# One weight half instead of three is split between the routing and the first expert, and after that expert's rows

## The chip, the cores and the metric

One core of one Trainium2 chip runs the whole program as one launch. The metric is the device time of that core in microseconds. The kernel before was timed three times: 524.74, 525.13 and 525.47 us, with a median of 525.13 us. One further execution was profiled.

## The reference, cut to what matters

```
attn: per head h, block of 64:  out = (q k^T * D) v + (q * lam^(i+1)) S ;  S = lam^64 S + (k * lam^(63-j))^T v
x     = attn as 1536 rows of 512
moe : e(t) = argmax(x w_gate), g = softmax weight of e(t);   row t = g * relu(x w1[e]) w2[e]     (8 experts, 512 -> 1024 -> 512)
moe2: out = (sigmoid(x w_g) * (x w_v)) w_out                                                     (512 -> 1536 -> 512)
```

All inputs are float32. The output is 1536 rows of 512.

## The kernel before, in words

The program has three stages: the attention with the routing, the eight experts, and the gated MLP. Each engine runs its own instructions in the order in which the program text issues them (`manual_schedule`, line 75), so the place of a call in the text sets the place of its instructions on every engine at once.

**Matmuls in fp16 pairs.** Every float32 factor of the expert stage is split into a high and a low fp16 part, and a product is three matmuls: high by high, low by high, and high by low. A weight therefore has to be split before TensorE can use it. A *chunk* is a quarter of one expert's weights (two chunks of `w1`, two of `w2`, four to an expert), and the program splits a chunk in two *halves* of 128 x 1024. Half n belongs to chunk n // 2, and expert e uses halves 8e to 8e+7, in this order. One half costs one operation on ScalarE, `hi` (line 170), one on VectorE, `lo` (line 171), and a load of 512 KB into one of five staging buffers `st` on SyncE's queue (line 150). The load of half n+5 is issued when `lo` of half n has ended (`wload`, lines 141 to 152).

**Who issues the splits.** `work32` (line 193) issues the next half of the queue. Halves 0 and 1 go into the attention loop at steps 8 and 9 (`T32`). `NB` halves are issued at line 713, between the routing and the first expert. After that, `weights()` (line 232) issues one half at each of nine places of an expert: after each of the four passes of its first layer, after `xtr_e` of the next expert, and twice in each of the two passes of its second layer. `need` (line 237) issues a half on the spot only if the program has not yet issued it; it does not look at whether it has ended. Eight buffers of `hi` and `lo` limit how far ahead the splits run (`usable`).

**One expert.** A pass of the first layer (lines 814 to 832, four of them) is 24 matmuls into a PSUM bank: for each of two output blocks, four with `hi`, four with `lo`, four with `hi` against the low part of the rows. ScalarE then writes `hh` and VectorE `hl`. Passes one and two use the first chunk, three and four the second. Then `xtr_e` (line 687) turns the next expert's rows: eight transposes on TensorE, two casts `xh` on ScalarE, two subtractions `xl` on VectorE. A pass of the second layer (lines 842 to 863, two of them) runs over f = 0 to 7 with three matmuls each (`hi`, `hi`, `lo`), first for one output block and then for another; f = 0 to 3 use the expert's third chunk and f = 4 to 7 its fourth, a half for each two f. ScalarE writes `yh` and VectorE `yl`.

**Around the change.** The routing ends with the lists of rows `gidx` (line 656). `gather(0)` (line 657) fetches the first expert's rows from DRAM by two indirect DMAs on GpSimd's queue, while VectorE finishes the gate weights and builds two diagonal matrices `diag` (line 712). Then come the three splits of line 713, then `xtr_e(0, diag)`, whose matmuls at line 703 turn the rows and apply the gates, and `gather(1)`. Lines 763 to 807 follow: some thirty small VectorE operations that order the six further experts by size and write the table `tab`. SyncE reads the experts' numbers from it (line 808) before it issues a load of a half of expert 2 or later. In expert 1, after its four passes, VectorE also runs `places()` and `further()` (lines 718 to 760).

Of the kernel before, what the change touches and what calls it, by code (L numbers as in the profile page):

```python
# [32 lines left out]
def kernel(  # L33
# [34 lines left out]

    T32, T64, TW, TE = (8, 9), 7, 6, 3

    NB, WARM = 3, (30, 14, 8, 20, 24)

    N64, N64G = 57, 3

# [118 lines left out]
    def work32():  # L193
        return start32()()
# [52 lines left out]
    def bank(kind, shape, name):  # L247
        turns[kind].append(turns[kind].pop(0))
        tag, bufs = turns[kind][-1]
        return ps.tile(shape, F32, tag=tag, bufs=bufs, name=name)  # L250
# [4 lines left out]
    def gather(e):  # L255
        if e < E:
            xg_t[e] = xgp.tile([128, 2, DM], F32, tag="xg", name="xg")
            for r, n in ((0, 128), (1, W[e] - 128)):
                nc.gpsimd.indirect_dma_start(
                    out=xg_t[e][0:n, r, :], out_offset=None, in_=rows_d[:, :],  # L260
                    in_offset=IndirectOffsetOnAxis(ap=gidx[0:n, r, e:e + 1], axis=0))
# [412 lines left out]
    with ExitStack() as mctx:  # L674
# [12 lines left out]
        def xtr_e(e, diag=None):  # L687
            if e >= E:
                return
            xg = xg_t.pop(e)  # L690
            n = W[e] - 128
            xps_t = []
            xh_t[e] = xw_p.tile([128, KD, C], F16, tag="xh", name="xh")[:, :, 0:W[e]]
            xl_t[e] = xw_p.tile([128, KD, C], F16, tag="xl", name="xl")[:, :, 0:W[e]]
            for c2 in range(KD // 2):
                xps_t.append(bank("x", [128, 2, C], "xps_e")[:, :, 0:W[e]])
            for r, k in ((0, 128), (1, n)):
                for c in range(KD):
                    x, y = xg[0:k, r, c * 128:(c + 1) * 128], xps_t[c // 2][:, c % 2, r * 128:r * 128 + k]
                    if diag is None:  # L700
                        nc.tensor.transpose(y, x, ident[0:k, 0:k])
                    else:
                        nc.tensor.matmul(y, lhsT=x, rhs=diag[0:k, r, 0:k], start=True, stop=True)
            for c2, xps in enumerate(xps_t):
                sl = slice(2 * c2, 2 * c2 + 2)
                nc.scalar.copy(xh_t[e][:, sl], xps)
                nc.vector.tensor_tensor(xl_t[e][:, sl], xps, xh_t[e][:, sl], op=ALU.subtract)


        diag = ct.tile([128, 2, 128], F32, name="diag")  # L710
        for r in range(2):
            nc.vector.tensor_scalar(out=diag[:, r], in0=ident, scalar1=gts[:, r, 0:1], scalar2=None, op0=ALU.mult)
        for _ in range(NB):
            work32()
        xtr_e(0, diag)
        gather(1)

        def places():

# [291 lines left out]
```

## Time and profile before

| | |
|---|---|
| median of three runs | 525.13 us |
| profiled execution, its own time | 523.29 us |
| its span, first to last instruction | 521.7 us |
| TensorE (PE) busy | 504.3 us, 97% |
| VectorE (DVE) busy | 306.7 us, 59% |
| ScalarE (ACT) busy | 222.5 us, 43% |
| GpSimd (POOL) busy | 69.9 us, 13% |

The profiled execution took 1.84 us less than the median, and 1.6 us of its time lie outside the span. Engines work side by side, so a busy share does not say what an operation costs. What counts is which engine waited for which, and when. PE's weight loads are listed apart as PEld, and an engine's sequencer as PEq, SPq and so on. A row of a timeline gives the start and the duration; the records of neighbours on one engine overlap by about a tenth of a microsecond, so the distance between starts says what one costs its engine.

### The profile page before, as it was taken

The page shows a single profiled execution, that of the slowest core. Times are in us where ns is not written, and L with a number is a line of the kernel's source. Part 1 is how long each engine was busy: PE and PEld are TensorE (multiplying, and loading weights), DVE is VectorE, ACT ScalarE, POOL GpSimd, SP SyncE. Part 2 cuts the span into 40 slices and gives each one's busy share as a digit, 9 for nine tenths or more (in the row PEclk, how much of TensorE's full clock was granted, in tenths as well). Part 3 has the DMA queues.
Part 4 walks back from the last instruction along what each step waited for, and adds up shares of the span by engine and source line. Part 5 has one row for each costly group of instructions (what it writes and reads, how often), then busy time and mean ns, then how long its engine had stood idle before and what let it go on. Part 6 is the DMA issues. An engine that isn't in the chain of part 4 may idle for free.

```text
span 521.7 us, 9789 instructions
## 1 busy us (share of the span) xinstructions
PE 504.3 (97%) x4013; PEld 338.8 (65%) x4014; DVE 306.7 (59%) x505; ACT 222.5 (43%) x328; POOL 69.9 (13%) x78
## 2 busy tenths in 40 slices
PE   7999997999999999979999999999999999999995
PEld 6888877999999999974444444444444444444442
DVE  5657867979978887853767766677677520000000
ACT  3554643865876787531533334443444310000000
POOL 3576414301201100000000000000000001101101
PEclk9999999999999999998999999999999999999999
DMA  9999965775989787220432222422340001001001
GB/s 171 211 235 276 299 229 192 223 259 188 322 278 322 265 282 240 79 87 1 136 107 82 83 78 92 151 82 80 92 151 1 0 1 40 26 35 41 34 28 40
DMA packets 67472, 72.28 MB, mean 139 GB/s; under 512 B 40218, under 2 KB 40218, under 8 KB 67424
## 3 DMA queue, kind: packets, MB, share of 16 engines
q1 hardware_dynamic: 65072, 65.04, 41.0%
q0 software_dynamic: 2208, 6.57, 3.6%
q8 instruction: 33, 0.54, 0.4%
q14 instruction: 15, 0.12, 0.1%
q10 hardware_dynamic: 144, 0.00, 0.0%
HBM read 65.31 MB, written 6.29 MB: 137 GB/s over the span
## 4 chain that ended last, share of the span: by engine, by line
PE 52%; issue 1%; DMA 1%; POOLq 0%; ACT 0%; ACTq 0%
PE gv_ps L956 36%; PE o_ps L975 16%; DMA out_dram<-osb,oidx 1%; POOLq L1006 0%; ACT osb L978 0%; ACTq L978 0%; POOLq L979 0%
## 5 line engine op out<-in xcount | busy, mean ns | idle before, releaser
L956 PEld LDWEIGHTS <-hi 128*128 128x128 f16 x576 | 56.4, 98 | 71.2 <-issue 3.6
L171 DVE SCALAR_TENSOR_TENSOR lo<-st,hi 128x1024 f16<-128x1024 f32 x64 | 77.8, 1233 | 13.8 <-ACT hi L170 13.7
L956 PE MATMUL gv_ps<-yh,hi 128*128 128x512 f16 x288 | 74.7, 382 | 3.0 <-PEq L872 3.0
L956 PE MATMUL gv_ps<-yh,lo 128*128 128x512 f16 x288 | 74.4, 381 | 0.0
L956 PE MATMUL gv_ps<-yl,hi 128*128 128x512 f16 x288 | 73.9, 379 | 0.0
L170 ACT ACTIVATE hi<-st 128x1024 f16<-128x1024 f32 x64 | 66.2, 1053 | 3.5 <-DMA st<-in_moe_w_dram 3.5
L851 PE MATMUL y_ps<-hl,hi 128*128 128x224 f16 (+6 forms) x256 | 64.6, 253 | 0.3 <-DVE hl L827 0.3
L851 PE MATMUL y_ps<-hh,hi 128*128 128x224 f16 (+6 forms) x256 | 64.6, 253 | 0.0
L851 PE MATMUL y_ps<-hh,lo 128*128 128x224 f16 (+6 forms) x256 | 64.6, 253 | 0.0
L979 POOL DMA_INDIRECT out_dram<-osb,oidx x12 | 11.7, 974 | 329.4 <-ACT osb L978 329.4
L975 PE MATMUL o_ps<-hi,uh 128*128 128x512 f16 x144 | 54.6, 379 | 0.0
L975 PE MATMUL o_ps<-lo,uh 128*128 128x512 f16 x144 | 54.6, 379 | 0.0
L975 PE MATMUL o_ps<-hi,ul 128*128 128x512 f16 x144 | 54.6, 379 | 0.0
L964 ACT CAST uh<-u 128x512 f16<-128x512 f32 x36 | 22.3, 618 | 70.4 <-DVE u L963 70.4
L956 PEld LDWEIGHTS <-lo 128*128 128x128 f16 x288 | 28.4, 99 | 34.6 <-issue 1.1
L975 PEld LDWEIGHTS <-uh 128*128 128x128 f16 x288 | 28.2, 98 | 34.0
L851 PEld LDWEIGHTS <-hi 128*128 128x128 f16 x512 | 47.7, 98 | 0.2
L823 PEld LDWEIGHTS <-hi 128*128 128x128 f16 x512 | 46.4, 98 | 0.7 <-issue 0.6
L978 ACT ACTIVATE osb<-o_ps 128x512 f32<-128x512 f32 x12 | 7.2, 597 | 85.3 <-PE o_ps L975 85.3
L965 DVE TENSOR_TENSOR ul<-u,uh 128x512 f16<-128x512 f32 x36 | 24.9, 692 | 24.6 <-ACT uh L964 24.6
L963 DVE SCALAR_TENSOR_TENSOR u<-gv_ps,sg 128x512 f32<-128x512 f32 x36 | 24.7, 687 | 23.6 <-PE gv_ps L956 18.6
L170 ACT ACTIVATE hi<-cv 128x1024 f16<-128x1024 f32 x18 | 19.0, 1055 | 35.0 <-DVE cv L219 35.0
(168 smaller groups left out, 725.3 us busy)
## 6 DMA issues: line engine op xcount, KB each, us to landing
st<-in_moe_w_dram SPq DMA_DIRECT2D x64, 512.0 KB, 5.5
st<-in_moe_w_gate_dram SPq DMA_DIRECT2D x6, 1024.0 KB, 5.3
st<-in_moe_w_val_dram SPq DMA_DIRECT2D x6, 1024.0 KB, 5.2
st<-in_moe_w_out_dram SPq DMA_DIRECT2D x6, 1024.0 KB, 4.9
q<-in_q_dram SPq DMA_DIRECT2D x12, 256.0 KB, 4.8
k<-in_k_dram SPq DMA_DIRECT2D x12, 256.0 KB, 5.1
v<-in_v_dram SPq DMA_DIRECT2D x12, 256.0 KB, 5.3
rows_d<-X SPq DMA_DIRECT2D x12, 256.0 KB, 4.9
```

The source lines that it names most:

```text
L170: nc.scalar.activation(out=hi, in_=w, func=AF.Copy, scale=SW)
L171: return lambda: nc.vector.scalar_tensor_tensor(out=lo, in0=w, scalar=SW, in1=hi, op0=ALU.mult, op1=ALU.subtract)
L823: nc.tensor.matmul(hp[:, j], lhsT=lw[w][:, c, fs], rhs=rx[:, c], start=(c == 0 and m == 0), stop=(c == KD - 1 and m == 2))
L851: nc.tensor.matmul(yp[:, j], lhsT=lw[w][:, f % 4, ds], rhs=rh[:, f], start=(f == 0 and m == 0), stop=(f == KF - 1 and m == 2))
L956: nc.tensor.matmul(p, lhsT=lw[w][:, c, fs], rhs=ry[:, c, ts], start=(c == 0 and m == 0), stop=(c == KD - 1 and m == 2))
L963: nc.vector.scalar_tensor_tensor(out=u, in0=banks[1], scalar=SU, in1=sg, op0=ALU.mult, op1=ALU.mult)
L964: nc.scalar.copy(uh[:, f, ts], u)
L965: nc.vector.tensor_tensor(ul[:, f, ts], u, uh[:, f, ts], op=ALU.subtract)
L975: nc.tensor.matmul(op, lhsT=lu[:, f, tsl], rhs=rw[w][:, f % 4, :], start=(f == 0 and m == 0), stop=(f == KF2 - 1 and m == 2))
L978: nc.scalar.activation(out=osb, in_=op, func=AF.Copy, scale=1.0 / (SX * SW * SW * SY * SW * SU * SW))
L979: nc.gpsimd.indirect_dma_start(out=out, out_offset=IndirectOffsetOnAxis(ap=oidx[:, t:t + 1], axis=0), in_=osb, in_offset=None)
```

## The change

`NB`, the number of halves split between the routing and the first expert, goes from 3 to 1. The one that is left is issued behind `xtr_e(0, diag)` and `gather(1)`, not ahead of them. Everything else stays, so all later places issue a half that stands two earlier in the queue.

```diff
-    NB, WARM = 3, (30, 14, 8, 20, 24)
+    NB, WARM = 1, (30, 14, 8, 20, 24)
...
         diag = ct.tile([128, 2, 128], F32, name="diag")
         for r in range(2):
             nc.vector.tensor_scalar(out=diag[:, r], in0=ident, scalar1=gts[:, r, 0:1], scalar2=None, op0=ALU.mult)
+        xtr_e(0, diag)
+        gather(1)
         for _ in range(NB):
             work32()
-        xtr_e(0, diag)
-        gather(1)
```

## Rows read from the trace of the kernel before

**Rows 1.** Busy time by engine, 88 to 108 us: length, PE, PEld, DVE, ACT, POOL.
```profile
88.00:108.00 20.00, 20.00 (x210) 20.00 (x210) 17.50 (x46) 13.21 (x19) 4.61 (x4) 1.00 0.80 261
```
**Rows 2.** Waits of PE: who waited for whom, us in total, times, longest.
```profile
PE gv_ps L956 <- PEq L872: 3.0, 1, 3.0
PE xps_e L703 <- DVE lo L171: 1.9, 2, 1.0
...
PE y_ps L851 <- DVE hl L827: 0.3, 1, 0.3
```
**Rows 3.** Timeline of PE, first experts: start, duration, operation, count, idle before it.
```profile
84.17 1.13 PE L703 MATMUL xps_e<-diag,xg 128*128 128x128 f32 x8 [0.97 <-DVE lo L171]
86.22 1.10 PE L703 MATMUL xps_e<-diag,xg 96*128 96x96 f32 x8 [0.92 <-DVE lo L171]
87.49 0.80 PE L823 MATMUL h_ps<-xh,hi 128*128 128x224 f16 x4 [0.17 <-ACT xh L706]
...
92.35 0.55 PE L823 MATMUL h_ps<-xh,hi 128*128 128x224 f16 x4
...
96.95 0.93 PE L701 MATMUL xps_e<-ident,xg 128*128 128x128 f32 x8
...
116.12 0.96 PE L701 MATMUL xps_e<-ident,xg 128*128 128x128 f32 x8
...
126.11 0.56 PE L823 MATMUL h_ps<-xh,hi 128*128 128x232 f16 x4
```
**Rows 4.** Timeline of DVE, the same stretch.
```profile
82.65 3.49 DVE L171 SCALAR_TENSOR_TENSOR lo<-st,hi 128x1024 f16<-128x1024 f32 x3
87.47 1.16 DVE L707 TENSOR_TENSOR xl<-xps_e,xh 128x448 f16<-128x448 f32 x2 [1.34 <-ACT xh L706]
88.55 0.16 DVE L764 SCALAR_TENSOR_TENSOR key<-cnt_s,c 128x6 f32<-128x6 f32 x1
...
92.41 0.62 DVE L827 SCALAR_TENSOR_TENSOR hl<-h_ps,hh 128x448 f16<-128x448 f32 x1
92.94 1.22 DVE L171 SCALAR_TENSOR_TENSOR lo<-st,hi 128x1024 f16<-128x1024 f32 x1
...
117.84 1.25 DVE L171 SCALAR_TENSOR_TENSOR lo<-st,hi 128x1024 f16<-128x1024 f32 x1
119.01 0.25 DVE L721 TENSOR_TENSOR cp<-oh_all,off_x 128x96 f32<-128x96 f16 x1
...
125.16 1.18 DVE L707 TENSOR_TENSOR xl<-xps_e,xh 128x464 f16<-128x464 f32 x2
126.25 2.35 DVE L171 SCALAR_TENSOR_TENSOR lo<-st,hi 128x1024 f16<-128x1024 f32 x2
```
**Rows 5.** Timeline of ACT, the same stretch.
```profile
86.91 0.98 ACT L706 CAST xh<-xps_e 128x448 f16<-128x448 f32 x2 [6.51 <-PE xps_e L703]
...
97.15 0.54 ACT L826 ACTIVATE hh<-h_ps 128x448 f16<-128x448 f32 x1 [0.52 <-PE h_ps L823]
97.59 1.05 ACT L170 ACTIVATE hi<-st 128x1024 f16<-128x1024 f32 x1
98.53 0.96 ACT L706 CAST xh<-xps_e 128x448 f16<-128x448 f32 x2
```
**Rows 6.** DMA issues and us to landing: `gather(0)`'s two parts, then all weight loads.
```profile
xg<-rows_d,gidx POOLq DMA_INDIRECT x1, 3.7
xg<-rows_d,gidx POOLq DMA_INDIRECT x1, 4.2
...
st<-in_moe_w_dram SPq DMA_DIRECT2D x64, 512.0 KB, 5.5
```
**Rows 7.** Timeline of SP (its queue's DMA issues) and POOL, 80 to 85 us.
```profile
81.87 0.94 POOL L259 DMA_INDIRECT xg<-rows_d,gidx  x1 [0.31 <-issue]
...
83.89 0.38 SPq L150 DMA_DIRECT2D st<-in_moe_w_dram  x1
```
**Rows 8.** Timeline of PE after its longest wait, the gated MLP's first matmuls.
```profile
234.84 1.87 PE L956 MATMUL gv_ps<-yh,hi 128*128 128x512 f16 x4 [3.03 <-PEq L872]
...
237.87 1.03 PE L956 MATMUL gv_ps<-yl,hi 128*128 128x512 f16 x4
238.73 1.03 PE L956 MATMUL gv_ps<-yh,hi 128*128 128x512 f16 x4
```

## The prediction

> **What bounds the kernel now.** I read the waits of PE first, then the timelines of PE, VectorE and ScalarE around 80 to 130 us, and the DMA issues last. PE is the bound: it is busy for all of the 20 us in which the first expert runs [rows 1], and the list of its waits [rows 2] holds just one of 3.0 us, at the branch ahead of the gated MLP, one of 1.9 us in two pieces at the first expert's rows, and a few tenths elsewhere. So whatever makes PE wait in the experts lengthens the run by as much, and a split that is taken off another engine gains nothing unless PE waited for it.
>
> The 1.9 us are put down to `lo` in that list. The reader should doubt this. `xtr_e(0)` reads `diag` and the gathered rows `xg`, and no split. Its two parts begin at 84.17 and 86.22 us [rows 3]. The gather's second DMA starts at 81.87 [rows 7] and lands 4.2 us later [rows 6], at 86.1, which is what the second part waits for; the first DMA, 3.7 us to landing, answers in the same way to the first part. The three `lo` end at 82.65 + 3.49 = 86.14 [rows 4], close by chance. After them VectorE is idle for 1.34 us until `xh` exists, and ScalarE is idle for 6.51 us before `xh` [rows 5]. The three splits of before are thus hidden in the wait for the gather.
>
> **The change part by part.** *Two halves fewer, and the third one moved.* What they cost before is nothing, so taking them out gains 0. The one thing that could be gained is the gather: three loads on SyncE's queue are set off by these `lo`, from 83.89 us on [rows 7], while the second DMA is under way. Bounds: 0, if they meet too late, and 0.9 us, PE's idle time before its second part [rows 3]; I take 0, since that load is issued only 2.2 us before the landing and itself needs 5.5 [rows 6].
>
> By the Trainium skill, "DMA: Bandwidth & Descriptors", section "Queues, rings and completion order", a DMA engine takes turns between the queues that have work for it, so the loads and the gather do share engines. If this is why the second DMA took 4.2 us and the first 3.7, the sum below is smaller by 0.5; it is weighed as a rival.
>
> *`gather(1)` ahead of the split.* It stands on GpSimd's queue, where the splits issue nothing, so it starts when it did: 0.
>
> *What the half that is left pushes.* Half 2 now stands behind `xh` on ScalarE and `xl` on VectorE. The second `xh` starts at about 87.4 and takes its engine to 87.8; `hi` ends at 88.9, `lo` runs from 88.9 to 90.1. Queued behind it on VectorE are the thirty small operations, 92.41 − 88.55 = 3.86 us [rows 4]: they end at 93.9 instead of 92.4. Behind them comes `hl` of the first pass, 0.53 us from start to start, and behind that the `lo` issued after the first pass.
>
> *First wait.* That `lo` is now half 3; before it was half 5. Half 3 belongs to the chunk that PE reads in its third pass. It runs from 93.9 + 0.5 = 94.4 to 95.65. The third pass starts at 92.35, and two passes of 24 matmuls last to 96.95 [rows 3], so a matmul is 0.096 us. Four with `hi` and two with `lo` later, at 92.93, PE wants half 3 and is held until 95.7: **+2.7**. Nothing behind it on PE can go ahead.
>
> *Second wait.* From 95.7 there are 18 matmuls left of the third pass (1.7 us) and 24 of the fourth (2.3): 99.7. Transposes of 0.8 bring the second layer to 100.5. Before, `hh` started 0.2 after the pass's end (96.95, 97.15 in rows 3 and 5), so now at 100.0, and `hi` of half 6 follows it by 0.44 and takes its engine 0.94 (97.59 to 98.53): 100.4 to 101.45. VectorE does `lo` of half 6 from 101.5 to 102.7. ScalarE does two `xh` (0.9) and `hi` of half 7, to 103.3; VectorE two `xl` (1.08) and `lo` of half 7, from 103.7 to 104.95. PE wants `lo` of half 6 at f = 4, 14 matmuls in, at 101.84: 0.9. It then wants `hi` of half 7 at 103.1 (0.2), and `lo` two matmuls later at 103.5: 1.4. Together **+2.5**. Before, the halves in these two slots were 8 and 9, which nobody wants until expert 1.
>
> *Third wait.* In expert 1 the same slot held half 17 and now holds 15, wanted at f = 6. In times of before: transposes at 116.12, second layer from 116.9, half wanted 20 matmuls later at 118.8; this `lo` ended at 119.1 [rows 4]: **+0.3**.
>
> *Fourth wait.* Then VectorE spends 119.01 to 126.25 on `places`, `further` and `xl`, and the next two `lo` end at 127.5 and 128.6 [rows 4]. Before they were halves 18 and 19, for expert 2's third pass; now they are 16 and 17, for its first, which starts at 126.11 [rows 3], with the third wait 126.4. PE wants half 16 four matmuls later at 126.8: 0.7; half 17 two after that, at 127.7: 0.9. Together **+1.6**.
>
> *What goes.* PE's wait of 0.3 us for `hl` in expert 2 [rows 2] has its cover then, since PE comes later: **−0.3**. From expert 3 on, nothing: an expert offers nine slots for eight halves, so the lead, three halves at the start instead of five, grows by one in each. The loads come later too (half 7's after half 2's `lo`, at 90.1 instead of 83.89), but at 5.5 us to landing it is there at 95.6 and ScalarE wants it at 102.3: 0. If it were late, the second wait would grow by as much. The last two halves end two slots later, in expert 6, where PE has no wait: 0.
>
> Sum: 2.7 + 2.5 + 0.3 + 1.6 − 0.3 = **+6.8 us**. The profiled execution would go from 523.29 to 530.1. The median of the runs shown is 1.84 above it, so I carry the difference over: 525.13 + 6.8 = **531.9 us**.
>
> **The rivals.**
>
> *PE's clock falls.* After the 3.03 us at the branch the first eight matmuls took 3.03 us, against 0.86 for four later [rows 8], the lower of its two levels (1.2 against 2.4 GHz) for a while: a loss of 3.03 − 1.73 = 1.3 us. The two waits of 0.97 and 0.92 us cost no such thing: four matmuls of 87.49 on are slow by `xh` and `xl` alone. A wait of 2.7 us lies nearer to 3.03, but PE did more just before it. Time: 533.2.
>
> *The gather gains 0.5*, as the rule above would have it: 531.4. For it speaks 4.2 against 3.7; against it, how late the loads start.
>
> *Only the first wait is real*, because the waiting of PE lets ScalarE and VectorE run ahead so that the halves of the second layer are in time: 525.13 + 2.7 − 0.3 = 527.5. Against it: `hi` of half 6 is queued behind `hh` of a pass that PE itself has made late.
>
> *The split still runs in the gap*, so that the change does less than it says: then `lo` of half 2 pushes nothing, the first wait shrinks by 90.1 − 88.6 = 1.5, and the time is 530.4. The text's order on ScalarE speaks against it.
>
> *Hidden anyway*: PE gets halves 3, 6 and 7 in time. It would need VectorE to be 2.7 us ahead of the rows above: 525.1.
>
> *Faster.* The list of waits is right and `lo` does hold `xtr_e(0)`. Then PE starts up to 1.9 us earlier, and the time is 523.2. It decides only if half 3's `lo`, which moves with it, also ends before the third pass reaches it, at 92.93 less 1.9; the thirty small operations stand in its way, and by the landings PE waited for the gather.
>
> **How the numbers follow.** Forecast 0.46; clock 0.18; gather 0.12; only the first wait 0.11; split in the gap 0.04; hidden 0.04; faster 0.05. Around the forecast alone, with a tenth or two on each of seven ends, the range is 531.0 to 532.8. The range that should hold 8 in 10 takes in the clock, once or twice in part, at the top and the first wait alone at the bottom: 527.3 to 534.0. A difference of 0.2% (1.05 us) is about what a measurement of this kernel can tell from no change. Faster by more than that: 0.05; within: 0.04; slower: 0.91.
>
> **What would show it.** On PE, a wait at line 823 for `lo` of about 2.7 us at 93 us, two or three at line 851 that sum to 2.5 us at 102 to 105, and about 1.6 us at line 823 near 132, all released by VectorE's line 171. PE's parts at line 703 should start at the same times, with other work or none named as releaser. The thirty operations should begin near 90.05. The prediction is wrong if PE's third pass runs through, if line 703 starts more than 0.3 us earlier, or if the granted clock of PE is below full anywhere between 90 and 135 us.

## The result and the profile after

| | before | after |
|---|---|---|
| median | 525.30 us (524.74 to 527.74, 4 runs) | 533.12 us (531.15 to 533.53, 4 runs) |
| profiled execution, its own time | 523.29 us | 533.53 us |

The changed kernel is slower: the ratio is 1.0131, with a 95% interval of 1.0099 to 1.0163. The forecast of 531.9 us is 1.2 us short of the median, which lies inside the range. The figure of the rival in which PE's clock falls, 533.2 us, is nearer, and the clock did fall.

The list of PE's waits after the change (who waits for whom, us in total, times, longest):

```profile
PE h_ps L823 <- DVE lo L171: 3.9, 3, 2.6
PE gv_ps L956 <- PEq L872: 3.2, 1, 3.2
PE y_ps L851 <- DVE lo L171: 2.0, 2, 1.3
...
PE xps_e L703 <- DVE cnt_s L665: 1.5, 1, 1.5
PE xps_e L703 <- DMA xg<-rows_d,gidx: 0.2, 1, 0.2
```

Against [rows 2], the rows for `lo` at line 823 (first layer) and line 851 (second layer) are new, 5.9 us in five waits, and `lo` has gone from line 703. PE's timeline shows where they lie (start, duration, operation, count, idle before it):

```profile
84.85 1.16 PE L703 MATMUL xps_e<-diag,xg 128*128 128x128 f32 x8 [1.49 <-DVE cnt_s L665]
86.21 1.10 PE L703 MATMUL xps_e<-diag,xg 96*128 96x96 f32 x8 [0.20 <-DMA xg<-rows_d,gidx]
87.48 0.80 PE L823 MATMUL h_ps<-xh,hi 128*128 128x224 f16 x4 [0.17 <-ACT xh L706]
...
92.34 0.55 PE L823 MATMUL h_ps<-xh,hi 128*128 128x224 f16 x4
92.72 0.35 PE L823 MATMUL h_ps<-xh,lo 128*128 128x224 f16 x2
95.69 0.44 PE L823 MATMUL h_ps<-xh,lo 128*128 128x224 f16 x2 [2.61 <-DVE lo L171]
95.91 0.95 PE L823 MATMUL h_ps<-xl,hi 128*128 128x224 f16 x4
...
104.39 0.27 PE L851 MATMUL y_ps<-hh,lo 128*128 128x224 f16 x1 [0.73 <-DVE lo L171]
...
106.58 0.27 PE L851 MATMUL y_ps<-hh,lo 128*128 128x224 f16 x1 [1.28 <-DVE lo L171]
...
126.11 0.27 PE L851 MATMUL y_ps<-hh,lo 128*128 128x224 f16 x1 [0.15 <-issue]
...
134.48 0.37 PE L823 MATMUL h_ps<-xh,lo 128*128 128x232 f16 x2 [0.52 <-DVE lo L171]
135.62 0.37 PE L823 MATMUL h_ps<-xh,lo 128*128 128x232 f16 x2 [0.76 <-DVE lo L171]
```

The first expert starts where it did (87.48, against 87.49 in [rows 3]), and its third pass too (92.34 against 92.35). Six matmuls later PE stands for 2.61 us. The matmuls from 95.91 on take 0.95 us for four instead of 0.55. The windows say why (length, busy time of PE, PEld, DVE, ACT and POOL, granted clock, DMA share, GB/s):

```profile
92.00:96.00 4.00, 1.39 (x15) 1.11 (x13) 3.81 (x17) 2.71 (x4) 2.19 (x2) 0.98 0.39 122
96.00:100.00 4.00, 4.00 (x27) 3.38 (x26) 1.57 (x3) 0.86 (x2) 0.49 (x1) 0.59 0.69 204
...
244.00:248.00 4.00, 4.00 (x11) 1.32 (x9) 0.00 (x0) 0.00 (x0) 0.00 (x0) 0.50 0.00 0
```

In [rows 1] the granted clock is 1.00 throughout. Now it is 0.59 in the window behind the wait: PE runs at the lower of its two levels, 1.2 GHz instead of 2.4. Means of 0.98 and 0.59 over two windows of 4 us stand for (0.02 + 0.41) x 4 / 0.5 = 3.4 us at that level. The last row is the branch ahead of the gated MLP, where, counted in the same way, the lower level lasted 6.8 us; before, 3.4 us (0.76 in the window from 232 to 236 us and 0.81 from 236 to 240). VectorE's timeline shows who was late:

```profile
84.14 0.17 DVE L665 COPY cnt_s<-cnt 128x8 f32<-128x8 f32 x1 [1.12 <-PE warm L340]
...
88.87 1.23 DVE L171 SCALAR_TENSOR_TENSOR lo<-st,hi 128x1024 f16<-128x1024 f32 x1 [0.25 <-ACT hi L170]
90.01 0.16 DVE L764 SCALAR_TENSOR_TENSOR key<-cnt_s,c 128x6 f32<-128x6 f32 x1
...
93.88 0.62 DVE L827 SCALAR_TENSOR_TENSOR hl<-h_ps,hh 128x448 f16<-128x448 f32 x1
94.41 1.22 DVE L171 SCALAR_TENSOR_TENSOR lo<-st,hi 128x1024 f16<-128x1024 f32 x1
...
103.10 1.23 DVE L171 SCALAR_TENSOR_TENSOR lo<-st,hi 128x1024 f16<-128x1024 f32 x1 [0.32 <-ACT hi L170]
...
124.80 1.25 DVE L171 SCALAR_TENSOR_TENSOR lo<-st,hi 128x1024 f16<-128x1024 f32 x1
```

This is [rows 4] with everything from `key` on 1.46 us later (90.01 against 88.55), and the `lo` that starts at 94.41 is now half 3, which PE wants at once. The `lo` at 103.10 is half 6 and ends at 104.33, and PE goes on at 104.39. The `lo` at 124.80 is half 15 and ends at 126.05. PE's matmul at 126.11 takes it, though the profile names no releaser there; this is the third wait. In the experts ScalarE has no wait for a load before 171.9 us, so no weight came late from DRAM in these waits.

The balance goes by marks: how much later the same matmul starts in the profiled execution of after than in that of before.

| mark | later by, us | added since the mark above |
|---|---|---|
| expert 0, first layer | -0.01 | |
| expert 0, second layer | 4.44 | 2.77 first wait, 1.67 lower clock |
| expert 1 | 6.97 | 2.53 second wait |
| expert 2, first layer | 7.29 | 0.33 third wait |
| expert 2, second layer | 8.92 | 1.63 fourth wait |
| expert 3 | 8.45 | -0.47, the wait for `hl` that went |
| end of the experts | 8.44 | 0.00 |
| gated MLP | 8.59 | 0.15 |
| its last product | 10.24 | 1.65, longer lower clock at the branch |

The 1.67 us are what remains of the step of the second mark when the 2.77 us by which the third pass was held are taken off. A bracket of the timeline counts idle time from the modelled end of the matmul before, a mark counts from start to start, so the same wait is 0.1 to 0.5 us longer in this table. The waits come to 2.77 + 2.53 + 0.33 + 1.63 - 0.47 = 6.79 us.

### The profile page after: what moved, and what is told of

It is laid out like the page before. It is cut to its first block, busy times and chain, and to the rows that moved or that the text cites. A ratio compares the mean times of both kernels' runs of the same rounds, so it can differ in the third digit from the quotient of the medians.

```text
span 532.0 us, 9789 instructions
## 1 busy us (share of the span) xinstructions
PE 509.5 (96%) x4013; PEld 340.2 (64%) x4014; DVE 307.4 (58%) x505; ACT 222.1 (42%) x328; POOL 67.1 (13%) x78
## 4 chain that ended last, share of the span: by engine, by line
PE 52%; issue 1%; DMA 1%; POOLq 0%; ACT 0%; ACTq 0%
PE gv_ps L956 36%; PE o_ps L975 16%; DMA out_dram<-osb,oidx 1%; POOLq L1006 0%; ACT osb L978 0%; ACTq L978 0%; POOLq L979 0%
## 5 line engine op out<-in xcount | busy, mean ns | idle before, releaser
L823 PE MATMUL h_ps<-xh,lo 128*128 128x224 f16 (+6 forms) x256 | 34.2, 255 | 3.9 <-DVE lo L171 3.9
```

The costliest lines, as they stand in the source:

```text
L823: nc.tensor.matmul(hp[:, j], lhsT=lw[w][:, c, fs], rhs=rx[:, c], start=(c == 0 and m == 0), stop=(c == KD - 1 and m == 2))
```

## The experiments

The theory: what counts is the lead of the splits over PE, set mainly by the number; the place adds delay to the first wait alone; and the lower clock behind that wait is a cost of its own. The rivals: the place alone makes the loss; the clock costs nothing since PE would wait for the next half anyway; every half costs its share.

Each ratio is against runs of the kernel before in the same job, on the same chip. e1 to e4 share 29 of them (median 525.38 us, 522.99 to 528.27), e5 to e8 share 13 (524.06 us).

**The changed kernel again.** No edit.

> The changed kernel once more, as the mark for the others on this chip. Its trace shows 8.4 us more up to the end of the experts: 6.8 us of waits for splits and 1.7 us of half clock after the first of them, and another 1.7 us of half clock after the branch. If all of that recurs, 533.1 (7.5 to 8.5 above the kernel before); if the clock falls in some executions only, 530.5 to 533.5 with a spread of over 1 us.

Measured: 532.52 us (531.2 to 534.2, 6 runs), ratio 1.013 [1.009, 1.0169]. It is 7.1 us above the 525.38 of before. The same waits stand in its trace (2.61, 0.73 and 1.28 us in expert 0). Its windows show that the clock fell a second time there, after the 1.28 us:

```profile
96.00:100.00 4.00, 4.00 (x27) 3.27 (x26) 1.74 (x3) 1.00 (x2) 0.51 (x1) 0.57 0.66 208
...
104.00:108.00 4.00, 2.31 (x14) 1.56 (x15) 3.69 (x5) 1.85 (x2) 1.03 (x2) 0.79 0.84 289
108.00:112.00 4.00, 4.00 (x35) 3.66 (x34) 0.37 (x1) 0.95 (x2) 0.00 (x0) 0.79 0.72 251
```

**The number alone**: one half, at the old place.

```diff
-    NB, WARM = 3, (30, 14, 8, 20, 24)
+    NB, WARM = 1, (30, 14, 8, 20, 24)
```

> One half in place of three, but at its old place ahead of the first expert's rows. Theory (the lead of the splits over PE is too short, and the moved half pushes the thirty table operations by 1.5 us on top): the table operations begin at 88.55 as before, the first wait shrinks from 2.6 to 1.1 us, the second (2.0), third (0.15) and fourth (1.3) stay: 4.7 to 5.0 us above the kernel before, 530.2. The clock should not fall after a first wait of 1.1 us; if it does, 531.9. Rival (the new place is what costs): no wait of over 0.5 us at line 823, 525.3.

Measured: 528.48 us (526.88 to 531.04, 12 runs), ratio 1.0056 [1.0031, 1.0082]. PE's timeline in the first expert:

```profile
93.89 0.37 PE L823 MATMUL h_ps<-xh,lo 128*128 128x224 f16 x2 [1.15 <-DVE lo L171]
...
100.93 0.27 PE L851 MATMUL y_ps<-hh,lo 128*128 128x224 f16 x1 [0.73 <-issue]
...
103.13 0.27 PE L851 MATMUL y_ps<-hh,lo 128*128 128x224 f16 x1 [1.28 <-DVE lo L171]
```

The second-layer waits are the same 0.73 and 1.28 us as after the whole change, and by marks the second, third and fourth wait add 2.53, 0.34 and 1.63 us, each within 0.01 of the whole change. Only the first differs: 1.15 us of waiting (1.30 by the marks) instead of 2.61 (2.77), and PE's clock stays full in the experts. So the number makes 5.3 us of the waits, counted from the start of expert 0 to the end of the experts, and the order makes the other 1.47 and leads to the lower clock. The time rose by 3.1 us only; a rise of 4.8, to 530.2, was expected. The profile of before that the count starts from is better by 0.86 us than a second one (e10 below). What makes up the rest of the difference is not shown.

**The order alone**: three halves, behind `xtr_e(0, diag)` and `gather(1)`.

```diff
-        for _ in range(NB):
-            work32()
         xtr_e(0, diag)
         gather(1)
+        for _ in range(NB):
+            work32()
```

> Three halves as before, but all three behind the first expert's rows. Theory: halves 2 to 4 run on VectorE from 88.9 to 92.3, the table operations end 3.4 us later, and PE meets the first expert's second layer with hl two times about 1.1 us late, no wait for lo: 2.2 us above the kernel before, 527.5, clock full. Rival (the number alone costs): 525.3. Rival (the place is what costs most): over 530.

Measured: 526.19 us (524.85 to 527.29, 12 runs), ratio 1.001 [0.9986, 1.0034]: a loss of 0.8 us that can't be told from none, less than expected. In the trace the experts take 2.30 us longer than in the first profile of before: 1.13 us in the first layer, at the lower clock, and 1.17 us in a new wait in two pieces, PE for `hl` of the last pass, which stands behind the three splits on VectorE. PE's timeline, and then a window:

```profile
84.56 2.20 PE L703 MATMUL xps_e<-diag,xg 128*128 128x128 f32 x16 [1.49 <-DVE cnt_s L665]
...
101.27 0.26 PE L851 MATMUL y_ps<-hl,hi 128*128 128x224 f16 x1 [0.93 <-DVE hl L827]
```

```profile
86.00:90.00 4.00, 3.84 (x24) 2.97 (x23) 2.84 (x4) 3.67 (x5) 0.00 (x0) 0.57 0.17 49
```

No half is late, so the rival that the place alone makes the loss falls. PE's clock fell here too, after the 1.49 us ahead of line 703; in the changed kernel the same idle time of 1.49 us, in the row at 84.85 above, was followed by full clock. So the length of the wait alone does not decide whether the clock falls.

**The first wait filled**: the changed kernel, with 44 matmuls of no use ahead of the third pass of expert 0. Nothing reads their results.

```diff
+                if e == 0 and fp == 2:
+                    warm(44, tag="st", bufs=1)
```

> The changed kernel with 44 small matmuls of no use (128 x 128 on constants, 55 ns each, 2.4 us) ahead of the third pass of expert 0, where PE waits for half 3 anyway. The waits stay as long as the splits need, so the third pass still goes on at 95.7. Theory (the half clock after the first wait is a cost of its own, 1.7 us, caused by PE's standing still): the granted clock stays full up to the branch, the experts end 1.5 to 1.8 us earlier than in the changed kernel, 531.4. Rival (the clock would have fallen anyway, or the loss is VectorE's and not PE's): the end of the experts as in the changed kernel or later, 533.1 or more.

Measured: 529.99 us (527.99 to 533.35, 12 runs), ratio 1.0087 [1.0056, 1.0117], 2.5 us below e1; the two intervals overlap, so the trace has to decide. Its windows, where the changed kernel had 1.39 and 4.00 busy at a clock of 0.98 and 0.59:

```profile
92.00:96.00 4.00, 3.85 (x59) 3.60 (x57) 3.84 (x17) 2.71 (x4) 2.55 (x2) 1.00 0.36 114
96.00:100.00 4.00, 4.00 (x44) 4.00 (x43) 2.78 (x3) 1.93 (x3) 0.13 (x1) 1.00 0.77 234
```

The clock stays full, the later waits are the same 0.73 and 1.28 us, and from the start of expert 0 (87.13 here) to the end of the experts this kernel is 6.77 us behind before, 6.42 by the mark and 0.35 for its earlier start. The changed kernel is 8.46 behind. The difference of 1.69 is the clock, a cost on top of the wait, and what remains agrees with the 6.79 of waits. All executions together point the same way: their mean granted clock has a median of 0.996 over the 12 runs of this kernel and of 0.988 over the six of e1.

**The thirty small operations behind the first pass**: the changed kernel, with lines 763 to 809 moved into expert 0, so that half 3's `lo` need not wait for them.

```diff
-        key = ct.tile([128, ES], F32, name="key")
...
+                if e == 0 and fp == 0:
+                    key = ct.tile([128, ES], F32, name="key")
...
```

> The changed kernel with the thirty small table operations issued after the first pass of expert 0 and its split, not ahead of that expert. Theory (half 3 is late because the table stands ahead of it; VectorE's total is what binds, so the wait moves on): no wait over 0.3 us at the third pass; the table runs from about 92.9 to 96.8, and PE meets the halves 4 to 7 late in the second layer of expert 0, several waits of together 4.4 us; the later waits of 0.15 and 1.3 stay: 5.8 us above the kernel before without a fall of the clock, 531.2, and 532.9 with one. Rival (the place of the table is the fault, the lead of the splits is enough): only the old second wait of 2.0 is left, 529.

Measured: 532.1 us (529.22 to 534.8, 4 runs), ratio 1.0139 [1.0102, 1.0175] against 524.06 for before in the same job; no gain. PE's timeline in the second layer of expert 0:

```profile
100.06 0.27 PE L852 MATMUL y_ps<-hh,lo 128*128 128x224 f16 x1 [0.36 <-DVE lo L171]
...
101.73 0.27 PE L852 MATMUL y_ps<-hh,lo 128*128 128x224 f16 x1 [0.92 <-DVE lo L171]
...
103.40 0.27 PE L852 MATMUL y_ps<-hh,lo 128*128 128x224 f16 x1 [0.92 <-DVE lo L171]
...
105.60 0.37 PE L852 MATMUL y_ps<-hh,lo 128*128 128x224 f16 x1 [1.33 <-DVE lo L171]
```

The wait in the third pass is gone. The second layer now holds PE four times, 3.53 us together, where the changed kernel held it for 0.73 + 1.28. Most of the wait was moved, not taken away: VectorE has the same work to do up to the last half of the expert, and PE, held no longer in the third pass, finds the next halves late instead. All waits for `lo` come to 5.0 us here and to 5.9 in the changed kernel. What is saved there goes to the clock in this execution: by the windows PE ran at the lower level for 3.4 us after two waits of 0.96 us at line 703 (0.50 from 88 to 90 us), and for 6.8 us from the last waits of the second layer on (0.50 from 104 to 110). So no gain in time is shown, and one that the clock hides is not ruled out.

**The lead given back**: the changed kernel, with two halves ahead of `xtr_e(0, diag)` and one behind.

```diff
+        for _ in range(2):
+            work32()
         xtr_e(0, diag)
         gather(1)
         for _ in range(NB):
             work32()
```

> Two halves split ahead of the first expert's rows as before, the third behind them as in the changed kernel; so the lead is that of the kernel before and the place that of the changed one. Theory (the moved half costs only what its lateness and the push of 1.5 us do to halves that PE wants soon, and with a lead of five none of them is wanted soon): no wait of over 0.4 us in expert 0, 525.4 (within 0.3% of the kernel before). Rival (the place costs by itself, by the 1.5 us that the table comes later): 526.5 to 527.

Measured: 523.68 us (521.64 to 525.36, 10 runs) against 524.06 (13 runs), ratio 0.9991 [0.9976, 1.0006]. PE's waits hold no row for `lo` at all; the longest in the experts is

```profile
PE y_ps L853 <- DVE hl L829: 0.3, 1, 0.3
```

as in [rows 2]. The place of the one half thus costs nothing that can be measured once the other two are back.

**Two halves at the old place.** This asks whether each half costs a share of the 3.1 us of e2, or whether there is a lead that suffices.

```diff
-    NB, WARM = 3, (30, 14, 8, 20, 24)
+    NB, WARM = 2, (30, 14, 8, 20, 24)
```

> Two halves in place of three, at the old place ahead of the first expert's rows: a lead of four. Theory (a lead costs only where it falls under what PE wants next: a threshold): a wait of about 0.3 us for half 7 in expert 0's second layer and of 0.8 for half 17 in expert 2, none at the third pass of expert 0, and the old wait of 0.3 goes: 0.5 to 0.8 us above the kernel before, within 0.2% of it. Rival (each half that is missing costs the same, half of what number_only added up to the end of the experts): 2.5 us above.

Measured: 524.66 us (523.28 to 525.86, 10 runs) against 525.34 (13 runs), ratio 0.9983 [0.996, 1.0005]. One wait for `lo` of 0.65 us is left, in expert 2. The share theory falls: the third half's removal cost nothing that can be measured, the second's cost all of it.

**`places` and `further` two experts later**: the changed kernel with both moved from expert 1 to expert 3, to test the account of the fourth wait.

```diff
-            if e == 1:
+            if e == 3:
```

> The changed kernel with places and further (6.2 us of VectorE) issued in expert 3, not in expert 1. Theory: the fourth wait (0.52 and 0.76 us at line 823 in expert 2) goes, as halves 16 and 17 no longer stand behind them, and no new wait comes in expert 3 or 4, where the lead is seven halves: 1.3 to 1.6 us less than the changed kernel up to the end of the experts. Rival (the lead alone decides): the wait in expert 2 stays at over 1 us, or an equal one comes in expert 4.

Measured: 534.74 us (2 runs), ratio 1.0207 [1.0178, 1.0237]. The fourth wait went, as expected: expert 3 starts 6.63 us later than before instead of 8.45. That no new wait would come was wrong. PE's timeline in expert 4:

```profile
181.99 0.25 PE L851 MATMUL y_ps<-hh,hi 128*128 128x204 f16 x1 [0.56 <-ACT hh L826]
...
183.34 0.25 PE L851 MATMUL y_ps<-hl,hi 128*128 128x204 f16 x1 [1.11 <-DVE hl L827]
...
185.10 0.33 PE L851 MATMUL y_ps<-hl,hi 128*128 128x204 f16 x1 [1.08 <-DVE hl L827]
```

These are 2.75 us for `hh` and `hl`, followed by 3.4 us at the lower clock, and the end of the experts is 11.15 us later than before. Here no half is late for PE. Instead ScalarE waits for loads, and `hh` stands behind the `hi` that waits. Its timeline, and then the window behind the moved block:

```profile
176.00 1.06 ACT L170 ACTIVATE hi<-st 128x1024 f16<-128x1024 f32 x1 [2.06 <-DMA st<-in_moe_w_dram]
...
180.48 1.06 ACT L170 ACTIVATE hi<-st 128x1024 f16<-128x1024 f32 x1 [1.81 <-DMA st<-in_moe_w_dram]
```

```profile
168.00:172.00 4.00, 4.00 (x47) 4.00 (x45) 3.66 (x17) 2.05 (x4) 0.00 (x0) 1.00 0.08 31
```

`places` and `further` now keep VectorE from 164.69 to 170.56 us. No `lo` ends meanwhile, so no load is issued: from 168 to 172 us the DMA share is 0.08, against 0.93 in the same window of the changed kernel. The loads behind the block then come late. So a block of some 6 us on VectorE also holds the loads that its splits set off, and PE feels it some 11 us after its end. This chain is read from one trace; no run took a link of it away.

**The branch filled**: the kernel before with 40 matmuls of no use behind the last product of the experts, to see whether PE's longest wait can be given work as in e4.

```diff
+        warm(40, tag="st", bufs=1)
```

> The kernel before with 40 small matmuls of no use behind the last of the experts' stage, ahead of the branch. In the kernel before PE stands still for 3.0 us there and its clock is at half for 3.4 us after it in the profiled execution, worth 1.7 us; over many executions the mean granted clock goes from 0.981 to 1.0. Theory (the standing still lets the clock fall): they run while the sequencer fetches past the branch, the still time shrinks from 3.0 to about 1, the clock stays full at the branch: 0.5 to 2 us less than before, 523.2 to 524.9. Rival (the branch starts only when the queue ahead of it has drained): the still time stays at 3.0 and 2.2 us are added, 527.5.

Measured: 527.27 us (526.69 to 528.32, 4 runs), ratio 1.0069 [1.0043, 1.0095], slower. PE's timeline:

```profile
233.38 2.39 PE L340 MATMUL warm<-ones 128*128 128x128 f16 x40 [0.94 <-DVEq L873]
...
238.46 1.87 PE L957 MATMUL gv_ps<-yh,hi 128*128 128x512 f16 x4 [2.68 <-PEq L873]
```

The filler ran, and after it PE still stood for 2.68 us for its own sequencer, and its first four matmuls took 1.87 us as in [rows 8]. It looks as if the branch begins for PE only when PE has run out of work, so that matmuls ahead of it push it back; no run separated this further.

**The kernel before, profiled a second time**, because e2 and e9 cost less than expected.

> The kernel before once more, for a second profile. In all traces but its first one the two diag operations start at 83.9 to 84.5 us, in its own at 82.25. If that comes from the three splits that stand behind them, they start near 82.3 here too; if it is an accident of one execution, they start near 84 here, and the three lo after them end at 87.5 or later, and so does xl.

Its time was 525.49 us, against 523.29 of the first profile. VectorE's timeline, and PE's:

```profile
84.33 0.53 DVE L712 TENSOR_SCALAR diag<-ident,gts 128x128 f32<-128x128 f32 x2
84.78 3.49 DVE L171 SCALAR_TENSOR_TENSOR lo<-st,hi 128x1024 f16<-128x1024 f32 x3
88.19 1.14 DVE L707 TENSOR_TENSOR xl<-xps_e,xh 128x448 f16<-128x448 f32 x2
```

```profile
88.85 0.35 PE L823 MATMUL h_ps<-xl,hi 128*128 128x224 f16 x2 [0.36 <-DVE xl L707]
...
89.38 0.35 PE L823 MATMUL h_ps<-xl,hi 128*128 128x224 f16 x2 [0.18 <-DVE xl L707]
```

Here the three `lo` start 2.13 us later than in [rows 4], at 84.78, last until 88.27, and push `xl` to 88.19 (87.47 in [rows 4]). PE waits for it, and the second layer of expert 0 starts 0.86 us later, counted from the start of the first. The gap ahead of `xl` that the prediction took for cover was there in the first execution and not in this one. The trace of e8, whose program is the kernel before up to the end of the experts, is a third sample: there, too, PE waits for `xl` (0.39 and 0.18 us), and the second layer starts 0.89 us later.

**Do two halves beat three?** The kernels of e6 and e9 again.

> Two halves ahead of the first expert's rows and one behind, in more executions. The second profile of the kernel before shows VectorE at diag at 84.3 us, so that three lo end at 88.3 and push xl by 0.8 us, for which PE waits 0.5 us in its first pass; two lo end at 87.1 and push nothing. Theory: 0.5 to 0.9 us less than the kernel before (ratio 0.9983 to 0.999), with an interval that may just miss 1. Rival (the push is of no weight over many executions): ratio 1.000 within 0.0006.

> Two halves only, at the old place, in more executions. Theory: it saves the same 0.5 to 0.9 us at xl, pays 0.65 us for half 17 in expert 2 and saves 0.3 to 0.5 there later: 0.3 to 0.7 us less than the kernel before (ratio 0.9987 to 0.9995), not as good as two ahead and one behind. Rival (fewer halves are slower in any number): 0.5 us or more above the kernel before.

Measured against 523.88 us (23 runs): 524.4 us (12 runs) for two early and one behind, ratio 1.0001 [0.9979, 1.0022]; 524.69 us (12 runs) for two alone, ratio 1.0005 [0.9983, 1.0027]. Neither beats the kernel before, and the small advantages of e6 and e9 did not come back. The 0.5 to 0.9 us that the first was expected to gain lie inside its interval, so they are neither shown nor ruled out.

## Why the prediction was right, and where it was not

**The four waits and the sum.** Forecast +2.7, +2.5, +0.3, +1.6 and -0.3; by the marks +2.77, +2.53, +0.33, +1.63 and -0.47. The sum of 6.8 us came out as 6.79. The chain behind the first wait held in its steps: `key` began at 90.01 (forecast 90.05), `lo` of half 3 at 94.41 (94.4), and PE was released at 95.69 (95.7). The steps that the sum was built from, the `lo` of 1.2 us, the thirty operations of 3.86 and the matmul of 0.096, came from [rows 3, 4] and did not change, which is why it holds to a tenth. e2 shows the second to fourth wait with the number alone. e6 shows that all four go when two halves are given back, e9 that one half given back leaves 0.65 us of the fourth, and e7 that the fourth hangs on `places` and `further`. One reading of the list of PE's waits was too short: besides the rows that the prediction names it holds 1.8, 1.7 and 0.7 us in the attention stage, which the change does not touch.

**The clock: a step that failed.** The prediction said that it would be wrong if the granted clock of PE were below full anywhere between 90 and 135 us. It was 0.59 from 96 to 100. The likeliest case thus did not come true as it was stated: what came is the first rival, priced at 1.3 us and 533.2 us with a chance of 0.18. It cost 1.67 us by the marks, and e4 took off 1.69 by keeping PE at work through the wait. The price of 1.3 us was low for its own example: it counts the first eight matmuls behind the branch, and the windows of before show the lower level there for 3.4 us, worth 1.7. The argument against the case was that PE "did more just before it" than ahead of the branch. No row bore that out. In all three traces with this first wait at 2.6 us (the changed kernel, e1 and e7) the clock fell, so the case should have had the larger chance.

**What the splits cost before: mis-sized.** The prediction took the three splits to be hidden, a removal worth 0, by a gap of 1.34 us in [rows 4]. In e10 that gap is gone and the splits hold the first expert for about 0.9 us, and so they do in e8. In 11 of the 14 traces VectorE comes to `diag` only at 83.65 to 84.45 us, as in e10, and earlier in three (the first profile of before, e11 and e12), so the late case seems to be the usual one. Then the changed kernel gains about 0.9 us against the usual execution of before. The median was forecast by carrying 6.8 from a profile to the median, and the terms left out have opposite signs: 6.8 of waits, less about 0.9, plus about 1.7 of clock gives 7.6 us. This is an estimate: the 0.9 us stand in traces, and the medians of e11 could not confirm them. The 7.1 of e1 and the 7.8 of the first comparison lie on both sides. That the forecast of 6.8 came so near to these is in part luck, as the two terms cancel in part.

**The rivals.** *The gather gains 0.5*: the second part of line 703 starts at 86.21, before at 86.22 and in e10, with three halves as well, at 86.04, so no gain is seen. The Trainium skill's rule that a DMA engine takes turns between the queues that have work for it ("DMA: Bandwidth & Descriptors", section "Queues, rings and completion order") is not put in doubt by this, but no run here shows it deciding the gather. *Faster, the list of waits is right*: that list had named `lo` for line 703 [rows 2]. After the change no `lo` stands there, the second part starts at the same time, and its releaser is now the gather's DMA. The first part starts 0.68 us later than in [rows 3], behind VectorE, and this is covered by the second. *Only the first wait*: the second layer's 0.73 and 1.28 us are there. *The split in the gap*: it ran at 88.87, behind `xl`. *Hidden anyway*: PE waited 2.61 us.

**What stays open.** In the profiled execution the branch had the lower clock for 6.8 us instead of 3.4, which is 1.65 us of the 10.24 by which its last product comes later. e1's trace has 3.4 us there with the same program, so this belongs to the execution and not to the change. In e10 the lower clock lasts 6.8 us at the branch as well, with the kernel before. What decides whether PE's clock falls after a short wait is not settled.

## What to carry to other kernels

A split that no one waits for where it stands can still be the lead that later work lives on: count for every slot behind it which piece now falls there and when it is wanted, and the sum of the waits can come out to tenths of a microsecond, as here. The lead needed was a threshold: the third of three halves was worth nothing that could be measured, the second 3 us. A wait of some microseconds on TensorE is to be priced with and without the lower clock behind it, here 1.7 us, and a gap of one profiled execution is no safe cover until a second one shows it too.

## What was not expected of the hardware

**The clock after short waits.** In the profiled executions it fell after the wait of 2.6 us in all three traces that have it, after 1.49 us in e3 (window 86 to 90 at 0.57) and after two waits of 0.96 us in e5. It did not fall after the 1.49 us at the same line in the changed kernel, nor after 0.97 and 0.92 us in [rows 3]. After the 1.28 us in expert 0 it fell in e1 and not in the first profile of the same kernel, nor in e2. At the branch it fell in 13 of 14 traces, after PE had stood for 2.7 to 3.4 us; in e2 PE stood there for 3.02 us, as long as in [rows 8], and the clock stayed full.

**The kernel before spreads by 1%.** Its 29 runs of one job go from 522.99 to 528.27 us. Five with a mean granted clock of 0.999 took 522.99 to 523.37 us, four with 0.981 took 527.66 to 527.89. One pair of profiles can therefore be compared by marks within the traces, not by end times.

**VectorE and GpSimd around the gather.** `cnt_s` starts at 84.14 in the changed kernel, with 1.12 us idle before it, though the matmuls that write its source had ended by 82.0; in [rows 4] its successor `diag` had begun at 82.25. GpSimd's timeline of the changed kernel, and then that of two halves at the old place (e12):

```profile
83.27 0.96 POOL L259 DMA_INDIRECT xg<-rows_d,gidx  x1 [0.30 <-issue]
84.54 0.91 POOL L259 DMA_INDIRECT xg<-rows_d,gidx  x1 [0.30 <-DMA xg<-rows_d,gidx]
```

```profile
83.24 0.95 POOL L259 DMA_INDIRECT xg<-rows_d,gidx  x1 [0.30 <-issue]
84.50 1.92 POOL L259 DMA_INDIRECT xg<-rows_d,gidx  x1 [0.31 <-DMA xg<-rows_d,gidx]
```

In the first, `cnt_s` starts 0.09 us before the gather instruction of 83.27 ends (84.23). In the second, VectorE had begun `diag`, the last of its small operations, at 82.87, and its two `lo` ran from 83.27 to 85.64; the gather instruction that began inside them took 1.92 us instead of 0.91. In the 14 traces four gather instructions began inside a row of `lo`, and they took 1.59 or 1.92 us. The first of the four instructions of a trace took 1.17 us everywhere, all others 0.91 to 0.98. So each engine seems to hold the other, whoever comes first. By the Trainium skill, "SBUF — State Buffer", section "Who interferes with whom", VectorE and GpSimd share one pair of ports, and a VectorE instruction with two inputs in SBUF contends for it with a GpSimd instruction that reads SBUF. The longer gather instructions under `lo` agree with this: `lo` reads `st` and `hi`, and the gather reads its row numbers `gidx`. The late `cnt_s` does not follow from it, as it copies one input out of PSUM. No run took the cause away, so all this is argued and not shown. Such holding would explain why the three splits of before were hidden in one profile and not in the other.
